# Reordering the first three groups of a gated linear recurrence with an MLP behind it

## The chip, the cores and the metric

The kernel runs on one NeuronCore of a Trainium2 chip. Its time is the device time of one execution in microseconds, as the median of several runs. Five engines work beside each other, each in the order of its own queue: TensorE (PE in the profile, its weight loads PEld), VectorE (DVE), ScalarE (ACT), GpSimd (POOL) and SyncE (SP). SP does no arithmetic here; it issues DMA transfers, one after the other, and a transfer that must wait holds up those behind it.

## The reference

Shapes are fixed: batch 4, 8 heads, 768 steps, head dimension 48. The bridge makes of it 3072 tokens of width 384, and the second block has width 2048.

```python
mag = np.sqrt(a_re * a_re + a_im * a_im)
scale = np.minimum(mag, 0.999) / (mag + 1e-06)
a_re_n, a_im_n = (a_re * scale, a_im * scale)
for t in range(S):
    ar, ai = (a_re_n[:, :, t, :, None], a_im_n[:, :, t, :, None])
    new_re = ar * S_re - ai * S_im
    new_im = ar * S_im + ai * S_re
    kv = np.einsum('bhd,bhe->bhde', k[:, :, t], v[:, :, t])
    S_re, S_im = (new_re + kv, new_im)
    y[:, :, t] = np.einsum('bhd,bhde->bhe', q[:, :, t], S_re)
...
x = np.ascontiguousarray(attn_out.transpose(0, 2, 1, 3)).reshape(B * S, H * D)
h = x @ w_in
g = h * np.cos(h)
return (g @ w_out).astype(np.float32)
```

## The kernel before, in words

The 3072 tokens are cut into 24 chunks of 128 steps, and two chunks make a group: 12 groups, numbered from 0. `PEG` is 2: groups 0 and 1 are handled in one way at two places, the others in another.

For each group the following steps run, in this order of data.

- *Logarithms* (`logs`, `g_log`): ScalarE squares re and im, VectorE adds them into `lg`, then logarithms and exponentials give the log of the gate's size (in `lg`) and the tangent of half its angle (in `tan`). `mag`, `rs` are scratch. `load` fetches re and im of the next group.
- *Products* (`prods`, `g_prod`): a running sum over the 128 steps is a matmul with the constant triangle `sums`; its result is named `lgs`. Two exponentials give P (kept in the tile `lg`) and Q. VectorE forms q times P and k times Q. P's last row is sent to memory (`row`) and read back as a column per head (`end`); SP issues both. `load` fetches k and q of the next group.
- *Angles and phases* (`g_angle`, `g_phase`): an arctangent, then a running sum by matmuls named `phs`, and the whole turns are taken off.
- *Keys* (`keys`, `g_trig`, `g_stack`): sine and cosine, and from them `ks` and `qs`, 96 numbers per head and step.
- *Turning* to kT and qT, which have the 96 numbers on partitions. In groups 0 and 1 TensorE does it (`turned`, `f_turn`, matmuls `tp` against `ident`, copied by ScalarE). In later groups VectorE transposes blocks (`tr`) and DMA does the rest through memory (`moved`, then four transfers kT and one qT).
- *Chunks* (`chunks`): scores `sc` (VectorE masks them into `atm`), the state's update `sp`, and the output of the recurrence. In groups 0 and 1 that is `f_rows` (matmuls `yr`, copied to `rows`) and `f_columns` (three transposes `xp`, copied to xT). In later groups it is `f_out` (matmuls `yp`, two heads side by side, copied to `yT`) and `f_xt`, which turns it by DMA through memory (`x`, then xT).
- *The MLP*: `first` is 48 matmuls `hp` from xT and w_in with a gate each pair on ScalarE and VectorE (`gate`, `junk`); `second(g, i)` is 16 matmuls `op` of chunk i with w_out.

The weights come as 64-bit numbers. `convert` fetches each part by GpSimd's queue and makes 32-bit floats of it: two VectorE steps (L599, L601), one on ScalarE (L603, `low`) and one more on VectorE (L604). There are 12 parts of w_in and 16 of w_out, and they are interleaved with the first groups. In every later group GpSimd and the others check weights for numbers out of range.

The order of work is written down in calls of `weave`. Each takes several lists of steps with two bounds between 0 and 1, spreads each list evenly between its bounds, and runs all steps sorted by place. TensorE's and GpSimd's instructions keep that order, since `chain` makes each follow the last; ScalarE's do for the special functions (`special`), while its other instructions and all of VectorE's and SP's are placed by the scheduler of the language, by readiness. The weaves are: one for group 0's preparation; one with group 0's chunks and its `first`, and group 1's preparation; one with group 0's `second`, group 1's turning, chunks and `first`, and group 2's preparation; and then one for each n from 2, in which group n's chunks, group n-1's `second`, group n+1's preparation and group n's `first` come together.

Of the kernel before, what the change touches and what calls it, by code (L numbers as in the profile page):

```python
# [486 lines left out]
def fast_path(ctx, tc, q, k, v, a_re, a_im, moe_w_in, moe_w_out, out, least, odd, wide):  # L487
# [48 lines left out]
    X = [dict() for _ in range(NG)]  # L536
    Y = [dict() for _ in range(N)]

    PEG = 2

    def load(g, names, i=None):
        for name in names:
# [91 lines left out]
    def matmul(out, **kw):  # L634
        chain(nc.tensor.matmul(out, **kw), "tensor")  # L635

    tables = {AF.Ln: "natural_log_exp_and_others", AF.Exp: "natural_log_exp_and_others",
              AF.Arctan: "trig_and_small", AF.Sin: "trig_and_small"}
    loaded = [None]
# [20 lines left out]
    def g_log(g, i, n):  # L660


        x = X[g]
        re, im = cut(x["re"], i, n), cut(x["im"], i, n)
        if i == 0:
            for name in "lg", "tan", "rs", "mag":
                x[name] = temp(name, 2 if name == "tan" else 1)
        m2, sq, rs, mag = (cut(x[name], i, n) for name in ("lg", "tan", "rs", "mag"))
        nc.scalar.activation(out=m2, in_=re, func=AF.Square)
        nc.scalar.activation(out=sq, in_=im, func=AF.Square)  # L670
        nc.vector.tensor_tensor(out=m2, in0=m2, in1=sq, op=ALU.add)
        special(out=m2, in_=m2, func=AF.Ln, bias=tiny_b)
        special(out=mag, in_=m2, func=AF.Exp, scale=0.5)
        special(out=rs, in_=m2, func=AF.Exp, scale=-0.5)
        nc.vector.scalar_tensor_tensor(out=mag, in0=re, scalar=0.0, in1=mag,
                                       op0=ALU.max, op1=ALU.add)
        nc.vector.tensor_scalar(out=m2, in0=m2, scalar1=0.5, scalar2=math.log(CAP),
                                op0=ALU.mult, op1=ALU.min)
        special(out=rs, in_=rs, func=AF.Ln, scale=EPS, bias=one_b)
        special(out=sq, in_=mag, func=AF.Ln)  # L680
        special(out=sq, in_=sq, func=AF.Exp, scale=-1.0)
        nc.vector.tensor_tensor(out=m2, in0=m2, in1=rs, op=ALU.subtract)  # L682
        nc.vector.tensor_tensor(out=mag, in0=mag, in1=sq, op=ALU.mult)
        nc.vector.scalar_tensor_tensor(out=sq, in0=mag, scalar=2.0, in1=sq,
                                       op0=ALU.subtract, op1=ALU.mult)
        nc.vector.scalar_tensor_tensor(out=sq, in0=sq, scalar=-1.0, in1=im,
                                       op0=ALU.mult, op1=ALU.mult)
        nc.scalar.activation(out=rs, in_=re, func=AF.Relu, scale=-1.0,
                             accum_out=odd[:, ds(next(odds), 1)])

    def g_prod(g, i, n):


        x = X[g]
        if i == 0:
            x["P"], x["Q"] = x["lg"], temp("Q")
            x["row"] = rows_d.tile([G * DM], F32, tag="row", name="row")
            x["end"] = ft.tile([D2, G * H], F32, tag="end", name="end")
        for one in range(i, i + n):
            ps = pa.tile([C, DM], F32, tag="a", name="lgs")  # L700
            matmul(ps, lhsT=sums, rhs=cut(x["lg"], one, 1), start=True, stop=True)
            special(out=cut(x["P"], one, 1), in_=ps, func=AF.Exp)
            special(out=cut(x["Q"], one, 1), in_=ps, func=AF.Exp, scale=-1.0)
        u = cut(x["mag"], i, n)
        P, Q = cut(x["P"], i, n), cut(x["Q"], i, n)
        nc.vector.scalar_tensor_tensor(out=u, in0=Q, scalar=HUGE, in1=P,  # L706
                                       op0=ALU.min, op1=ALU.mult)
# [8 lines left out]
        nc.vector.tensor_scalar(out=end, in0=end, scalar1=-0.5, scalar2=None, op0=ALU.mult)  # L716
# [4 lines left out]
        nc.vector.tensor_tensor(out=P, in0=cut(x["q"], i, n), in1=P, op=ALU.mult)  # L721

    def g_angle(g, i, n):

# [27 lines left out]
    def g_stack(g, i, n):  # L752
        x = X[g]
        if i == 0:
            for name in "ks", "qs":
                x[name] = gt.tile([C, G * H, 2, D], F32, tag=name, name=name)
        for name, product in ("ks", "Q"), ("qs", "P"):
            for a, trig in enumerate(("cos", "sin")):
                nc.vector.tensor_tensor(  # L759
                    out=x[name][:, ds(i * H, n * H), a],  # L760
                    in0=cut(x[product], i, n).rearrange("p (x d) -> p x d", d=D),
                    in1=cut(x[trig], i, n).rearrange("p (x d) -> p x d", d=D), op=ALU.mult)
# [161 lines left out]
    def keys(g):  # L924
# [3 lines left out]
        for i, n in spans(g):  # L928
            yield lambda i=i, n=n: g_trig(g, i, n)
            yield lambda i=i, n=n: g_stack(g, i, n)  # L930
            for name in "kT", "qT":
                if g >= PEG:
                    yield lambda i=i, n=n, name=name: f_transpose(g, i, n, name)
                elif g == 0:
                    yield from turned(g, i, name)

    def turned(g, i, name):
        return [lambda hh=hh: f_turn(g, i, name, hh) for hh in range(2)]
# [14 lines left out]
    def chunks(g):  # L953
        for n in range(g * G, g * G + G):
            for hh in range(2):
                yield lambda n=n, hh=hh: f_scores(n, hh)
            yield lambda n=n: f_state(n)
            yield lambda n=n: f_out(n) if g >= PEG else f_rows(n)
            if g < PEG:
                yield lambda n=n: f_columns(n)  # L960
        if g >= PEG:
            yield lambda: f_xt(g)
        if g + 2 < NG:
            yield lambda: load(g + 2, ("v",))

# [13 lines left out]
    def guarded(g, count):  # L979
# [3 lines left out]
        for _ in range(min(count, len(guards))):  # L983
# [6 lines left out]
    after = stage.tile([1, 1], F32, tag="after", name="after", bufs=1)  # L990
    wait_for(X[0]["im"][0:1, G - 1, 0, 0:1])
    weave((logs(0), 0.0, 0.2), (prods(0), 0.2, 0.4), (each(g_angle, 0), 0.4, 0.5),
          (phases(0), 0.5, 0.6), (keys(0), 0.6, 1.0),
          (convert(into[:6]), 0.2, 1.0))
    weave((chunks(0), 0.0, 0.3), (logs(1), 0.0, 0.1), (convert(into[6:]), 0.0, 0.5),
          (first(0), 0.3, 1.0), (prods(1), 0.55, 0.57), (each(g_angle, 1), 0.58, 0.6),
          (phases(1), 0.75, 0.8), (keys(1), 0.8, 0.9), (convert(back[:8]), 0.5, 1.0))
    weave((convert(back[8:]), 0.0, 0.15), (second(0, 0), 0.0, 0.3),
          ([t for i in range(G) for name in ("kT", "qT") for t in turned(1, i, name)], 0.3, 0.4),
          (logs(2), 0.3, 0.35), (second(0, 1)[:2], 0.4, 0.5), (chunks(1), 0.4, 0.6),  # L1000
          (second(0, 1)[2:], 0.5, 0.6), (prods(2), 0.62, 0.63), (each(g_angle, 2), 0.63, 0.64),
          (first(1), 0.6, 1.0), (phases(2), 0.72, 0.75), (keys(2), 0.76, 0.9))
# [76 lines left out]
```

## Time and profile before

| what | us |
|---|---|
| runs, median (lowest to highest) | 757.03 (755.42 to 759.99) |
| the profiled execution | 759.09 |
| its span, from the first to the last instruction | 757.3 |
| TensorE busy in the span | 698.4 |
| VectorE busy | 397.8 |
| ScalarE busy | 392.3 |

The profiled execution is 2.06 us above the median, and 1.8 us of its time lie outside the span. The mean granted clock of TensorE is 0.972 of full speed. Times in the views are microseconds from the span's start. In the timeline a row has the start, the duration, the engine, the line, the operation, what is written from what, sizes and a count; in brackets stands how long the engine was idle before it, and what ended that. In the chain of work that ended last a row has the start, the duration, and the engine with the tile and line. In the list of waits a row has who waited for whom, the total in us, how often, and the longest. One matmul of 32-bit floats appears in the trace as two instructions, a transpose as one; the listings of the order below count matmuls.

### The profile page before, as it was taken

To read this page: it belongs to the slowest core of one execution; us is meant where nothing else is said; L and a number is where in the kernel's file an instruction comes from. 1 tells how busy PE (TensorE), PEld (TensorE's weight loads), DVE (VectorE), ACT (ScalarE), POOL (GpSimd) and SP (SyncE) were. 2 spreads that over 40 slices of the span, in tenths; PEclk is the share of its full clock that TensorE was granted. 3 is DMA by queue.
4 is the path that set the end of the run, shared out by engine and by line. 5 is a ranking of instruction groups with operands and counts; after the bars stand their busy time and mean duration, and the time that the engine had idled before them with its cause. 6 is when DMAs were issued, how large, how long until landed. Compare 5 with 4: busy or idle time off the path is not lost.

```text
span 757.3 us, 9367 instructions
## 1 busy us (share of the span) xinstructions
PE 698.4 (92%) x3540; PEld 525.3 (69%) x3540; DVE 397.8 (53%) x598; ACT 392.3 (52%) x727; POOL 32.2 (4%) x68
## 2 busy tenths in 40 slices
PE   1489969984999999999999999999999999999996
PEld 0287737773678678678687688687687687687773
DVE  5696972373274464465475366375465556541120
ACT  7485970354337347447557457457456456451230
POOL 2002100000000001001001001001001001000000
PEclk9997998896999999999999999999999999999998
DMA  9855521138244458558566566565574572270100
GB/s 276 200 147 163 150 85 30 35 98 151 73 124 97 115 142 187 122 146 191 121 159 190 120 143 164 116 150 153 116 177 126 126 167 86 62 167 22 43 1 26
DMA packets 231299, 93.96 MB, mean 124 GB/s; under 512 B 208318, under 2 KB 219713, under 8 KB 231244
## 3 DMA queue, kind: packets, MB, share of 16 engines
q1 hardware_dynamic: 224508, 67.76, 41.2%
q0 software_dynamic: 6016, 25.17, 9.6%
q8 instruction: 30, 0.49, 0.3%
q10 hardware_dynamic: 720, 0.33, 0.1%
q14 instruction: 25, 0.20, 0.1%
HBM read 68.82 MB, written 24.42 MB: 123 GB/s over the span
## 4 chain that ended last, share of the span: by engine, by line
PE 81%; DMA 6%; DVE 6%; ACT 3%; SPq 2%; issue 1%; POOL 0%; ACTq 0%; DVEq 0%
PE op L635 32%; PE hp L635 26%; PE sc L635 6%; PE yp L635 5%; PE sp L635 3%; PE phs L635 3%; DMA qT<-moved 3%; PE yr L635 2%; PE lgs L635 2%; SPq L777 1%; PE tp L789 1%; DVE w_out L604 1%; DVE w_out L601 1%; DVE ks L759 1%; DMA moved<-tr 1%
## 5 line engine op out<-in xcount | busy, mean ns | idle before, releaser
L635 PE MATMUL op<-w_out,gate 128*128 128x384 f32 x768 | 269.3, 498 | 3.0 <-DVE w_out L604 3.0
L635 PE MATMUL hp<-xT,w_in 128*128 128x256 f32 x1152 | 254.1, 382 | 0.6 <-ACT xT L850 0.6
L635 PEld LDWEIGHTS hp<-xT,w_in 128*128 128x128 f32 x1152 | 220.7, 192 | 34.6 <-ACT xT L850 1.0
L635 PEld LDWEIGHTS op<-w_out,gate 128*128 128x128 f32 x768 | 144.3, 193 | 101.8 <-DVE w_out L604 8.4
L894 DVE TENSOR_TENSOR gate<-hp,gate 128x512 f32<-128x512 f32 x96 | 65.7, 684 | 119.8 <-ACT gate L645 119.8
L895 ACT ACTIVATE junk<-hp 128x512 bf16<-128x512 f32 x96 | 57.3, 597 | 74.7 <-DVE gate L894 74.5
L645 ACT ACTIVATE gate<-hp,half_pi_b 128x512 f32<-128x512 f32 x96 | 65.6, 684 | 42.6 <-PE hp L635 42.6
L635 PEld LDWEIGHTS sc<-qT,kT 96*128 96x128 f32 x384 | 50.2, 201 | 24.7 <-issue 16.9
L635 PE MATMUL sc<-qT,kT 96*128 96x128 f32 x384 | 52.2, 287 | 15.7 <-DMA qT<-moved 13.9
L706 DVE SCALAR_TENSOR_TENSOR mag<-Q,lg 128x768 f32<-128x768 f32 (+1 forms) x13 | 11.6, 895 | 83.7 <-ACT Q L645 83.7
L808 DVE TENSOR_TENSOR atm<-sc,causal 128x512 f32<-128x512 f32 x48 | 33.0, 688 | 34.1 <-PE sc L635 34.1
L828 ACT COPY yT<-yp 48x512 f32<-48x512 f32 x40 | 23.1, 578 | 51.3 <-PE yp L635 51.0
L738 ACT CAST tan<-phs 128x384 int32<-128x384 f32 x24 | 11.5, 479 | 56.1 <-PE phs L635 56.1
L908 ACT ACTIVATE ot<-op 128x384 f32<-128x384 f32 x24 | 11.6, 483 | 47.1 <-PE op L635 47.1
L644 ACT ACT_TABLE_LOAD x26 | 33.4, 1283 | 3.5 <-issue 3.1
L635 PE MATMUL lgs<-lg,sums 128*128 128x384 f32 x48 | 19.3, 523 | 14.2 <-DVE lg L682 14.2
L635 PE MATMUL yp<-atm,v 128*48 128x128 f32 x320 | 30.4, 277 | 0.0
L635 PEld LDWEIGHTS sp<-v,ks 128*96 128x96 f32 x320 | 29.4, 165 | 0.6 <-issue 0.3
L635 PE MATMUL sp<-v,ks 128*96 128x48 f32 x320 | 29.6, 245 | 0.0
L615 ACT ACTIVATE e<-e,least_e_b 128x384 f32<-128x384 uint32 (+1 forms) x28 | 18.5, 660 | 18.8 <-DVE e L613 18.6
L739 DVE TENSOR_TENSOR tan<-phs,tan 128x384 f32<-128x384 f32 x24 | 13.4, 556 | 27.5 <-ACT tan L738 27.5
L635 PE MATMUL yp<-qT,state 96*48 96x128 f32 x272 | 26.5, 272 | 0.0
(93 smaller groups left out, 710.4 us busy)
## 6 DMA issues: line engine op xcount, KB each, us to landing
moved<-tr SPq DMA_DIRECT2D x20, 768.0 KB
raw<-in_moe_w_in_dram POOLq DMA_DIRECT2D x24, 512.0 KB, 6.1
raw<-in_moe_w_out_dram POOLq DMA_DIRECT2D x32, 384.0 KB, 4.0
kT<-moved SPq DMA_DIRECT2D x40, 192.0 KB
qT<-moved SPq DMA_DIRECT2D x10, 768.0 KB
re<-in_a_re_dram SPq DMA_DIRECT2D x24, 192.0 KB
im<-in_a_im_dram SPq DMA_DIRECT2D x24, 192.0 KB
k<-in_k_dram SPq DMA_DIRECT2D x24, 192.0 KB
```

What stands on the lines that cost most here:

```text
L615: nc.scalar.activation(out=e.bitcast(F32), in_=e, func=AF.Relu, scale=-1.0, bias=least_e_b, accum_out=odd[:, ds(next(odds), 1)])
L635: chain(nc.tensor.matmul(out, **kw), "tensor")
L644: chain(nc.scalar.preload_act_table_set(loaded[0]))
L645: chain(nc.scalar.activation(func=func, **kw))
L706: nc.vector.scalar_tensor_tensor(out=u, in0=Q, scalar=HUGE, in1=P, op0=ALU.min, op1=ALU.mult)
L738: nc.scalar.copy(out=ph.bitcast(I32), in_=ps)
L739: nc.vector.tensor_tensor(out=ph, in0=ps, in1=ph.bitcast(I32), op=ALU.subtract)
L808: nc.vector.tensor_tensor(out=y["atm"][:, ts(hh, HH)], in0=ps, in1=causal.unsqueeze(1).to_broadcast([C, HH, C]), op=ALU.mult)
L828: nc.scalar.copy(out=X[g]["yT"][half, :, i], in_=ps[half])
L894: nc.vector.tensor_tensor(out=gate, in0=ps, in1=gate, op=ALU.mult)
L895: nc.scalar.activation(out=junk, in_=ps, func=AF.Square, scale=1.0 / in_scale, accum_out=wide[:, ds(g * (NJ // 2) + jp, 1)])
L908: nc.scalar.mul(out=ot, in_=ps, mul=1.0 / (in_scale * out_scale))
```

## The change

Five things are changed.

1. `q` times P is written into the tile `mag` and not over P, and `g_stack` reads it there.
2. The two squares of `g_log` are put into ScalarE's chain, so they stay where the weave puts them.
3. `busy(count)` issues matmuls of 128 columns of the constants `ident` and `sums`, whose result nobody reads: six ahead of each of the two `lgs` of group 0, and eight ahead of its turning.
4. Group 1's output goes by `f_out` and `f_xt`, so by DMA; group 0 keeps `f_rows` and `f_columns`. Group 0's steps of turning and of its chunks are written out one by one.
5. The third weave is split in two. In the first half group 1's turning lies between the matmuls of `second(0, 0)`, then come group 1's chunks and in them group 2's products. In the second half `second(0, 1)` and group 2's phases and keys come before `first(1)`.

```diff
+    def busy(count):
+        ps = pa.tile([C, C], F32, tag="a", name="busy")
+        for _ in range(count):
+            matmul(ps, lhsT=ident, rhs=sums, start=True, stop=True)
...
-        nc.scalar.activation(out=m2, in_=re, func=AF.Square)
-        nc.scalar.activation(out=sq, in_=im, func=AF.Square)
+        chain(nc.scalar.activation(out=m2, in_=re, func=AF.Square))
+        chain(nc.scalar.activation(out=sq, in_=im, func=AF.Square))
...
+            if g == 0:
+                busy(6)
             ps = pa.tile([C, DM], F32, tag="a", name="lgs")
...
-        nc.vector.tensor_tensor(out=P, in0=cut(x["q"], i, n), in1=P, op=ALU.mult)
+        nc.vector.tensor_tensor(out=u, in0=cut(x["q"], i, n), in1=P, op=ALU.mult)
...
-        for name, product in ("ks", "Q"), ("qs", "P"):
+        for name, product in ("ks", "Q"), ("qs", "mag"):
...
-            yield lambda n=n: f_out(n) if g >= PEG else f_rows(n)
-            if g < PEG:
-                yield lambda n=n: f_columns(n)
-        if g >= PEG:
-            yield lambda: f_xt(g)
+            yield lambda n=n: f_out(n)
+        yield lambda: f_xt(g)
...
-          (phases(0), 0.5, 0.6), (keys(0), 0.6, 1.0),
-          (convert(into[:6]), 0.2, 1.0))
-    weave((chunks(0), 0.0, 0.3), (logs(1), 0.0, 0.1), (convert(into[6:]), 0.0, 0.5),
-          (first(0), 0.3, 1.0), (prods(1), 0.55, 0.57), (each(g_angle, 1), 0.58, 0.6),
+          (phases(0), 0.5, 0.6), (keys(0), 0.6, 0.9), (convert(into[:6]), 0.2, 1.0))
+    busy(8)
+    for t in (turned(0, 0, "kT") + turned(0, 0, "qT")
+              + [lambda: f_scores(0, 0), lambda: f_scores(0, 1)]
+              + turned(0, 1, "kT") + turned(0, 1, "qT")
+              + [lambda: f_state(0), lambda: f_rows(0), lambda: f_scores(1, 0),
+                 lambda: f_scores(1, 1), lambda: f_columns(0), lambda: f_state(1),
+                 lambda: f_rows(1), lambda: f_columns(1), lambda: load(2, ("v",))]):
+        t()
+    weave((logs(1), 0.0, 0.1), (convert(into[6:]), 0.0, 0.5),
+          (first(0), 0.2, 1.0), (prods(1), 0.55, 0.57), (each(g_angle, 1), 0.58, 0.6),
...
+    over = [t for i in range(G) for name in ("kT", "qT") for t in turned(1, i, name)]
+    weave((convert(back[8:]), 0.0, 0.3), (second(0, 0), 0.0, 0.65), (over, 0.2, 0.6),
+          (logs(2), 0.3, 0.31), (chunks(1), 0.7, 1.0), (prods(2), 0.85, 0.86),
+          (each(g_angle, 2), 0.86, 0.87))
+    weave((second(0, 1), 0.0, 0.35), (phases(2), 0.0, 0.1), (keys(2), 0.1, 0.4),
+          (first(1), 0.4, 1.0))
```

In the changed kernel the lines are some ten further down: L716 becomes L726, L721 becomes L731, L671 becomes L679, L894 becomes L904.

VectorE in group 0, before, from the second half's Q to the first wait for `end`. `mag`, `lg` and Q are the tiles above, and each row of 128x384 is one of the two chunks:

```order
L709 SCALAR_TENSOR_TENSOR Q<-mag,Q 128x384
L604 ISA w_in<-w_in,low 128x1024
L720 TENSOR_TENSOR Q<-k,Q 128x384
L739 TENSOR_TENSOR tan<-phs,tan 128x384
L601 SCALAR_TENSOR_TENSOR w_in<-raw,w_in 128x512
L747 TENSOR_SCALAR cos<-tan 128x384
L721 TENSOR_TENSOR lg<-q,lg 128x384 x2
L604 ISA w_in<-w_in,low 128x1024
L739 TENSOR_TENSOR tan<-phs,tan 128x384
L759 TENSOR_TENSOR ks<-Q,cos 128x8x48
L759 TENSOR_TENSOR ks<-Q,sin 128x8x48
L716 TENSOR_SCALAR end<-end 96x8
```

The same place in the changed kernel:

```order
L749 TENSOR_TENSOR tan<-phs,tan 128x384
L730 TENSOR_TENSOR Q<-k,Q 128x384
L731 TENSOR_TENSOR mag<-q,lg 128x384
L757 TENSOR_SCALAR cos<-tan 128x384
L601 TENSOR_SCALAR w_in<-raw 128x512
L749 TENSOR_TENSOR tan<-phs,tan 128x384
L603 SCALAR_TENSOR_TENSOR w_in<-raw,w_in 128x512
L769 TENSOR_TENSOR ks<-Q,cos 128x8x48
L606 ISA w_in<-w_in,low 128x1024
L769 TENSOR_TENSOR ks<-Q,sin 128x8x48
L769 TENSOR_TENSOR qs<-mag,cos 128x8x48
L726 TENSOR_SCALAR end<-end 96x8
```

The product with q moved up to where it is ready, and one `qs` product now stands ahead of the step on `end`.

TensorE from the `op` matmuls of group 0's first chunk to group 1's scores, before:

```order
L635 MATMUL op<-w_out,gate 128x384 x16
L789 MATMUL tp<-ident,ks 96x128 x8
L789 MATMUL tp<-ident,qs 96x128 x8
L789 MATMUL tp<-ident,ks 96x128 x8
L789 MATMUL tp<-ident,qs 96x128 x8
L635 MATMUL sc<-qT,kT 128x128 x4
```

And in the changed kernel:

```order
L637 MATMUL op<-w_out,gate 128x384 x4
L799 MATMUL tp<-ident,ks 96x128 x4
L637 MATMUL op<-w_out,gate 128x384 x4
L799 MATMUL tp<-ident,ks 96x128 x4
L799 MATMUL tp<-ident,qs 96x128 x8
L637 MATMUL op<-w_out,gate 128x384 x4
L799 MATMUL tp<-ident,ks 96x128 x8
L799 MATMUL tp<-ident,qs 96x128 x4
L637 MATMUL op<-w_out,gate 128x384 x4
L799 MATMUL tp<-ident,qs 96x128 x4
L637 MATMUL sc<-qT,kT 128x128 x8
```

The transposes moved in between the `op` matmuls; four of them are left behind the last.

TensorE around group 1's `hp`, before, from the last transposes of its output to group 2's first scores:

```order
L847 MATMUL xp<-ident,rows 128x128 x3
L635 MATMUL op<-w_out,gate 128x384 x4
L635 MATMUL lgs<-lg,sums 128x384 x2
L635 MATMUL hp<-xT,w_in 128x256 x18
L635 MATMUL phs<-tan,turns 128x384
L635 MATMUL phs<-tan,last 128x384
L635 MATMUL phs<-tan,turns 128x384
L635 MATMUL phs<-tan,last 128x384
L635 MATMUL hp<-xT,w_in 128x256 x30
L635 MATMUL sc<-qT,kT 128x128 x4
```

And in the changed kernel, from the last `yp` of group 1 (its `lgs` stand between the two halves of the scores before):

```order
L637 MATMUL yp<-qT,state 48x128 x2
L637 MATMUL phs<-tan,turns 128x384
L637 MATMUL phs<-tan,last 128x384
L637 MATMUL op<-w_out,gate 128x384 x4
L637 MATMUL phs<-tan,turns 128x384
L637 MATMUL phs<-tan,last 128x384
L637 MATMUL op<-w_out,gate 128x384 x12
L637 MATMUL hp<-xT,w_in 128x256 x48
L637 MATMUL sc<-qT,kT 128x128 x4
```

Group 2's `phs`, and all of the `op` of group 0's second chunk, now stand ahead of the whole of `hp`.

SP's queue at the same place, before, from group 2's `row` on:

```order
L712 DMA row<-lg 1x768
L715 DMA end<-row 48x16x1 x2
L549 DMA k<-in_k_dram 128x8x48 x2
L549 DMA q<-in_q_dram 128x8x48 x2
L774 DMA moved<-tr 128x1536 x2
L777 DMA kT<-moved 96x16x32 x4
L779 DMA qT<-moved 96x4x512
```

And in the changed kernel:

```order
L722 DMA row<-lg 1x768
L885 DMA x<-yT 48x4x256
L551 DMA k<-in_k_dram 128x8x48
L725 DMA end<-row 48x16x1 x2
L551 DMA k<-in_k_dram 128x8x48
L551 DMA q<-in_q_dram 128x8x48 x2
L885 DMA x<-yT 48x4x256
L551 DMA v<-in_v_dram 128x8x48
L889 DMA xT<-x 128x3x256
L784 DMA moved<-tr 128x1536
```

The two halves of group 1's output, `x`, came in around the loads of k and q, and xT after them.

More of the change, by code (lines that the diff above doesn't have):

```diff
@@ L537, in fast_path @@
     Y = [dict() for _ in range(N)]
-    PEG = 2
+    PEG, PER = 2, 1
     def load(g, names, i=None):
@@ L933, in keys @@
                     yield lambda i=i, n=n, name=name: f_transpose(g, i, n, name)
-                elif g == 0:
-                    yield from turned(g, i, name)
     def turned(g, i, name):
@@ L992, in fast_path @@
     weave((logs(0), 0.0, 0.2), (prods(0), 0.2, 0.4), (each(g_angle, 0), 0.4, 0.5),
-          (phases(0), 0.5, 0.6), (keys(0), 0.6, 1.0),
-          (convert(into[:6]), 0.2, 1.0))
-    weave((chunks(0), 0.0, 0.3), (logs(1), 0.0, 0.1), (convert(into[6:]), 0.0, 0.5),
-          (first(0), 0.3, 1.0), (prods(1), 0.55, 0.57), (each(g_angle, 1), 0.58, 0.6),
-          (phases(1), 0.75, 0.8), (keys(1), 0.8, 0.9), (convert(back[:8]), 0.5, 1.0))
[L998 to L1002, printed above, removed]
+          (phases(0), 0.5, 0.6), (keys(0), 0.6, 0.9), (convert(into[:6]), 0.2, 1.0))
[9 more added lines that the diff above has]
+          (first(0), 0.2, 1.0), (prods(1), 0.55, 0.57), (each(g_angle, 1), 0.58, 0.6),
+          (phases(1), 0.75, 0.8), (keys(1), 0.8, 0.9), (convert(back[:8]), 0.5, 1.0))
+    over = [t for i in range(G) for name in ("kT", "qT") for t in turned(1, i, name)]
[4 more added lines that the diff above has]
+          (first(1), 0.4, 1.0))
     for n in range(2, NG):
```

## The prediction

> **What bounds the kernel now.** I read the busy time by stretches first (columns: stretch in us, its length, busy us and instructions of TensorE, its weight loads, VectorE, ScalarE, GpSimd, then granted clock, DMA share, GB/s), with the stretches cut where TensorE's order changes kind.
>
> ```profile
> 24.20:30.09 5.89, 0.88 (x2) 0.00 (x0) 0.05 (x1) 0.00 (x0) 0.53 (x1) 1.00 1.11 246
> 30.09:61.30 31.21, 22.55 (x150) 21.15 (x150) 28.11 (x54) 22.14 (x36) 3.85 (x7) 0.92 0.52 130
> 61.30:89.40 28.10, 27.76 (x108) 22.25 (x109) 21.98 (x44) 22.12 (x42) 5.54 (x9) 0.90 0.66 179
> 89.40:104.30 14.90, 12.02 (x32) 5.00 (x30) 14.90 (x32) 9.44 (x16) 1.61 (x3) 1.00 0.31 98
> 104.30:111.90 7.60, 4.73 (x35) 3.74 (x35) 3.79 (x6) 7.57 (x14) 0.00 (x0) 0.96 0.07 26
> 111.90:144.40 32.50, 31.93 (x170) 25.17 (x171) 6.57 (x10) 4.69 (x11) 0.00 (x0) 0.80 0.19 38
> 144.40:168.70 24.30, 23.77 (x105) 19.49 (x103) 18.00 (x22) 15.68 (x31) 0.00 (x0) 1.00 0.29 71
> 168.70:181.70 13.00, 0.00 (x0) 0.01 (x1) 7.58 (x10) 8.97 (x14) 0.00 (x0) 0.65 1.13 210
> 181.70:757.30 575.60, 567.77 (x2934) 425.81 (x2934) 281.39 (x385) 284.70 (x536) 16.04 (x35) 0.99 0.50 120
> ```
>
> From 181.70 on TensorE is busy 567.8 of 575.6 us, and what it lacks lies after its last matmul. So TensorE bounds that part, and the change leaves its order there as it was. All that can move is when group 2's first `sc` starts, 181.73 now. Before it stand a front in which VectorE and ScalarE stop (24.20 to 30.09), a stretch in which VectorE has no free time (89.40 to 104.30, the conversions of w_out), and 13 us without a matmul. The waits of TensorE, then the front in order of time, then VectorE's waits between 34 and 104.3 and the last conversion say what ends each:
>
> ```profile
> PE lgs L635 <- DVE lg L682: 14.2, 2, 10.3
> PE sc L635 <- DMA qT<-moved: 13.9, 3, 13.0
> PE tp L789 <- DVE ks L759: 12.0, 2, 8.9
> ```
>
> ```profile
> 30.09 1.03 DVE L721 TENSOR_TENSOR lg<-q,lg 128x384 f32<-128x384 f32 x2 [5.84 <-DMA row<-lg]
> 30.73 0.84 ACT L670 ACTIVATE tan<-im 128x768 f32<-128x768 f32 x1 [7.49 <-DMA im<-in_a_im_dram]
> 33.84 0.16 DVE L716 TENSOR_SCALAR end<-end 96x8 f32<-96x8 f32 x1
> 33.98 1.94 PE L789 MATMUL tp<-ident,ks 128*96 128x128 f32 x8 [8.90 <-DVE ks L759]
> 34.46 0.55 DVE L759 TENSOR_TENSOR qs<-lg,sin 128x384 f32<-128x384 f32 x1
> 44.16 3.01 PE L635 MATMUL sc<-qT,kT 96*128 96x128 f32 x16
> 61.32 9.03 PE L635 MATMUL hp<-xT,w_in 128*128 128x256 f32 x28 [0.57 <-ACT xT L850]
> ```
>
> ```profile
> DVE gate L894 <- ACT gate L645: 4.9, 1, 4.9
> ```
>
> ```profile
> 104.37 0.91 PE L635 MATMUL op<-w_out,gate 128*128 128x384 f32 x2 [0.89 <-DVE w_out L604]
> 106.00 1.04 PE L789 MATMUL tp<-ident,qs 128*96 128x128 f32 x8
> ```
>
> **Front.** L721 wrote q times P over P, so it waited for the transfer that still read P. L670, the square of the next group's im, stood on ScalarE ahead of group 0's phase work and waited 7.49 us for its load. With a tile of its own and the squares chained behind, both stops go. What is late next is L726, which waits for the small transfer `end`. Its `row` is issued behind loads on SP that the change does not touch, so I leave it at 33.84. In the new order the last product `qs` stands right behind it: 33.84+0.16+0.55 is 34.6. Eight transposes at 1.04 to 1.94 us and a copy give `sc` at about 36 to 37, where before it came at 44.16, since it now goes ahead of the second chunk's transposes. From `sc` to the first `hp` took 17.2 us (44.16 to 61.32). The second chunk's 16 transposes now lie inside (2 to 4 us), but the same instructions at full clock save about as much. First `hp`: 53, against 61.32. The conversions that VectorE now does before the second half's logarithms push that half back some 4 us, under the wait for `end`.
>
> The constants are 20 matmuls of 128 columns, 40 instructions. At 3.01/16 = 0.19 us that is 7.5 us, in waits of 14.2 and 12.0 us, and no input waits for them. They cost nothing and may raise the clock.
>
> **To the last conversion.** VectorE's work is the same, and it ends the conversions at 104.3. From 30.09 to there it is free for 3.1+6.1+0 us. With some 2 us of work done earlier, the end could come at 94; with nothing regained, at 104.3. I take 102, near the upper row: the 4.9 us of the wait for the first gate shrink, but the new order still has gates, `end` and a whole group's logarithms ahead of the w_out conversions, each waiting on other engines. So of 8 us gained at the front, 6 are lost here.
>
> **Transposes of group 1.** All 32 now stand between the `op` matmuls that wait for conversions, so behind the last `op` (0.65) only four transposes (0.45) remain. `sc` of group 1 starts at 103.1, against 111.9. Their ScalarE copies now interleave with the conversions' ScalarE step, which leaves 14.90-9.44 = 5.5 us free there; in the next stretch before, the copies and a group's logarithms together took 7.57.
>
> **Group 1 and its output.** The rates come from the chain that ended last, in group 2 and later:
>
> ```profile
> 194.57 1.79 PE sc L635 x16
> 242.70 1.32 PE sp L635 x16
> 198.94 1.90 PE yp L635 x32
> 203.61 1.29 PE lgs L635 x4
> 213.28 1.29 PE phs L635 x4
> 204.90 5.16 PE op L635 x16
> 217.16 20.72 PE hp L635 x96
> ```
>
> From `sc` to the first `hp` of group 1 now stand, on TensorE, 32 `sc` (3.58), 32 `sp` (2.64), 64 `yp` (3.80), 4 `lgs` (1.29), 8 `phs` (2.58) and 32 `op` (10.32): 24.2 us, against 32.5. The 64 `yr` and 6 `xp` are gone, and with them a stretch whose granted clock is 0.80. So `hp` could start at 127.3, if xT is there. It now comes by DMA:
>
> ```profile
> 209.69 0.95 DVE L721 TENSOR_TENSOR lg<-q,lg 128x768 f32<-128x768 f32 x1
> 212.04 1.39 SPq L549 DMA_DIRECT2D q<-in_q_dram  x2
> 697.00 1.86 SPq L875 DMA_DIRECT2D x<-yT  x2
> 701.16 0.38 SPq L879 DMA_DIRECT2D xT<-x  x1
> ```
>
> ```profile
> 154.83 0.91 PE phs L635 x2
> 166.18 3.25 DMA moved<-tr
> 174.41 7.23 DMA qT<-moved
> 181.73 2.04 PE sc L635 x8
> 183.77 3.91 PE op L635 x8
> ```
>
> On SP the second half of x is now queued behind `k`, `end`, `k` and two `q` loads, and `q` waits for L731. `lgs` would end at 103.1+1.79+1.32+1.90+0.89+1.29 = 110.3. In group 3 the product of L721 ends at 210.64, 5.7 us after `lgs` (204.90); here the two `state` steps and an `atm` come between, so some 7.5: 117.8. Two q issues (1.39) put x at 119.2. No row gives the landing of x or xT; the nearest are `moved`, 3.25 us, and qT, 7.23 us, both through the same memory and larger or as large. The last group's two steps, 697.00 and 701.16, show the first within 4.2 us with its issues, near the lower one. So xT lands between 125.7 and 133.7. With 3.25 for x and 5, midway, for the strided xT it is 127.5, and a v load stands between them on SP. I take a wait of 1.3 us: `hp` at 128.6, ends 0 and 6.4. Behind xT on SP stand `moved`, kT and qT of group 2, whose `tr` is not ready before; it holds nothing up.
>
> **The 13 us.** Phases, keys and transposes of group 2 now come ahead of `hp` of group 1, which stays 20.72 us long without the `phs` inside. From the end of the last `phs` (155.74) to the landing of qT (181.64) took 25.9 us with gates between. Now the last `phs` ends at 110.3+0.89+1.32+1.90+2.58+2.58 = 119.6, so qT lands by 145.5, while TensorE reaches `sc` at 128.6+20.7 = 149.3. The stall is gone, with 3.8 us to spare; the cover is `hp` plus three quarters of an `op`.
>
> **Sum.** `sc` of group 2 at 149.3 instead of 181.73. The first instructions after the stall also ran slow: 2.04 us for 8 `sc` (0.90 at the rate above) and 3.91 for 8 `op` (2.58), 2.5 us that go too. 757.3-32.4-2.5 = 722.4 span. The profiled execution took 1.8 us more than its span and lies 2.1 us above the median of 757.03: predicted median 722.
>
> Steady groups: the squares, add and `mag` product change places but not number; L731's output no longer holds `lg`. I cost this at nothing: a group's `lgs` starts 13 us after its input L682 is done:
>
> ```profile
> 244.28 0.95 DVE L682 TENSOR_TENSOR lg<-lg,rs 128x768 f32<-128x768 f32 x1
> 258.27 1.29 PE lgs L635 x4
> ```
>
> **Rivals.** (a) *TensorE stays at half clock in the front.* Speaking for it: 1.94 us for 8 transposes at 33.98 against 1.04 at 106.00, and the clock falls to 0.92 and 0.90 around group 0's `yr`. Then the first `hp` comes at 58 to 60, the conversions end at 104 to 108, and the median is 724 to 728. The Trainium skill ("TensorE: Matmul & The Clock Gate", Part 1: The HAM clock gate) says that the array starts at half clock and is released only by some 3.4 us of sustained activity. By that rule 6 constants, 12 x 0.19 = 2.3 us, and 8, 3.0 us, are each too short to do it alone, and (a) would hold, 727; the trace agrees so far that 3.85 us of transposes at 33.98 did not release it. (b) *xT is late.* With 7.23 us for both steps `hp` waits 6.4 us: 727. Against it: the same two steps never stopped TensorE in ten later groups, though behind 40 `op` and 4 `lgs` where here 32 `op` stand. (c) *VectorE regains its free time*: conversions end at 96, 716. (d) *The stall moves and stays*: if the way from `phs` to qT takes over 29.7 us, each us more is lost; back in full it gives 735. Against it: for group 3 the way fits between the last `phs` (214.57) and the end of `hp` (237.88), 23.3 us, and the waits for qT other than the 13.0 add up to 0.9.
>
> (e) *Slower than before*: the squares now behind the last gate lengthen every group's logarithms by 2 x 0.84 + 0.95 = 2.6 us, and VectorE's add stands between the two `atm` products, so that `yp` could wait in each of 10 groups. The way to `lgs` decides only from 13 us more; to undo 35 us the add must cost `yp` 3.5 us a group, more than the 2.6 us that it is late.
>
> **Chances.** The forecast 0.55 (its own range 718 to 726), (a) 0.18, (b) 0.1, (c) 0.1, (d) 0.04, (e) 0.03. Range 713 to 731: it takes in (a), (b) and (c). A difference under 0.5%, 3.8 us, cannot be told here from no change; faster 0.96, same 0.01, slower 0.03.
>
> **What would show it.** VectorE has no wait for `row` and its wait for `end` ends near 33.8; first `hp` near 53; the last `op` of group 0 that waits for w_out near 102; no `yr` after 60; `hp` of group 1 at 127 to 130, with a wait named xT or none; no wait on `qT` at group 2's first `sc`, near 149; 573 us from there to the end. The forecast is wrong if `sc` of group 2 is not between 141 and 158, or if waits appear on TensorE after it.

## Result: 727.1 us against 756.2, and the profile after

The changed kernel takes 727.06 us (median; 725.74 to 727.43), the kernel before beside it 756.22 (755.41 to 759.99). The ratio is 0.960, interval 0.957 to 0.964: faster by 29 us. The forecast was 722, range 713 to 731. The profiled execution took 726.93 us, 725.1 of them in the span.

The stretches again, with the columns of the first table of the prediction, cut where TensorE's order changes kind:

```profile
24.20:31.00 6.80, 5.23 (x23) 3.14 (x23) 6.41 (x15) 4.30 (x8) 0.53 (x1) 0.82 0.98 208
31.00:37.30 6.30, 2.74 (x17) 2.19 (x17) 2.75 (x10) 2.49 (x5) 0.00 (x0) 0.70 0.88 179
37.30:56.65 19.35, 18.21 (x136) 17.51 (x135) 12.74 (x23) 12.92 (x20) 1.60 (x3) 0.76 0.31 89
56.65:82.40 25.75, 21.34 (x82) 16.84 (x82) 23.12 (x41) 21.13 (x39) 4.31 (x8) 0.90 0.64 166
82.40:91.00 8.60, 8.57 (x26) 6.74 (x27) 7.73 (x17) 4.74 (x8) 1.61 (x3) 0.67 0.83 206
91.00:104.98 13.98, 13.09 (x60) 8.43 (x59) 13.93 (x32) 12.93 (x24) 2.15 (x4) 1.00 0.34 114
104.98:106.17 1.19, 1.19 (x7) 0.86 (x8) 0.00 (x0) 1.16 (x2) 0.00 (x0) 1.00 0.00 0
106.17:130.76 24.59, 24.59 (x175) 18.28 (x174) 21.03 (x29) 13.55 (x23) 0.00 (x0) 1.00 0.58 122
130.76:151.48 20.72, 20.72 (x98) 18.24 (x97) 7.12 (x9) 10.12 (x22) 0.00 (x0) 1.00 0.68 162
151.48:725.10 573.62, 564.71 (x2935) 424.43 (x2933) 287.62 (x393) 292.35 (x550) 16.04 (x35) 1.00 0.50 121
```

The stretch without a matmul is gone: from 106.17 to 151.48 TensorE has no idle time. Group 2's first `sc` comes at 151.48, against 181.73, so 30.25 us of the 32.2 that the span lost are gained ahead of it; the rest lies in the slow start behind the old stall. But the last `op` that waits for w_out stands at 104.98, where it stood at 104.37 before. Up to there the change gained nothing, although the first `hp` comes 4.7 us earlier. The waits and the timeline rows that belong to it:

```profile
PE phs L637 <- DVE tan L749: 3.9, 1, 3.9
PE tp L799 <- DVE qs L769: 3.6, 1, 3.6
PE sc L637 <- DMA qT<-moved: 0.9, 2, 0.7
PE op L637 <- DVE w_out L606: 0.9, 1, 0.9
```

```profile
34.85 0.17 DVE L726 TENSOR_SCALAR end<-end 96x8 f32<-96x8 f32 x1 [3.55 <-DMA end<-row]
35.53 1.94 PE L799 MATMUL tp<-ident,qs 128*96 128x128 f32 x8 [3.56 <-DVE qs L769]
37.30 3.78 PE L637 MATMUL sc<-qT,kT 96*128 96x128 f32 x16
56.65 5.55 PE L637 MATMUL hp<-xT,w_in 128*128 128x256 f32 x15 [0.57 <-ACT xT L860]
82.42 1.65 PE L637 MATMUL phs<-tan,last 128*128 128x384 f32 x2 [3.92 <-DVE tan L749]
104.98 0.91 PE L637 MATMUL op<-w_out,gate 128*128 128x384 f32 x2 [0.89 <-DVE w_out L606]
106.17 1.95 PE L637 MATMUL sc<-qT,kT 96*128 96x128 f32 x16
```

VectorE waits for `end`, TensorE waits for the product that stands behind it there (35.53) and runs at half clock (16 `sc` in 3.78 us, where 1.95 is the time at 106.17). At 82.42 it waits 3.9 us for a small VectorE step.

### The profile page after: what moved, and what is told of

It reads as the page before. It is cut to its first block, busy times and chain, and to the rows that moved or that the text cites. A ratio compares the mean times of both kernels' runs of the same rounds, so it can differ in the third digit from the quotient of the medians.

```text
span 725.1 us, 9428 instructions
## 1 busy us (share of the span) xinstructions
PE 689.0 (95%) x3574; PEld 523.1 (72%) x3574; DVE 396.3 (55%) x598; ACT 393.3 (54%) x728; POOL 31.4 (4%) x68
## 4 chain that ended last, share of the span: by engine, by line
PE 85%; DMA 6%; DVE 5%; ACT 1%; issue 1%; SPq 1%; POOL 0%; DVEq 0%
PE op L637 33%; PE hp L637 29%; PE sc L637 6%; PE yp L637 5%; PE sp L637 4%; PE phs L637 4%; DMA qT<-moved 2%; PE lgs L637 2%; DMA end<-row 1%; DVE w_out L606 1%; DVE w_out L603 1%; PE yr L637 1%; PE tp L799 1%; DMA raw<-in_moe_w_in_dram 1%; DMA im<-in_a_im_dram 1%
## 5 line engine op out<-in xcount | busy, mean ns | idle before, releaser
L637 PE MATMUL op<-w_out,gate 128*128 128x384 f32 x768 | 262.6, 489 | 0.9 <-DVE w_out L606 0.9
L637 PEld LDWEIGHTS op<-w_out,gate 128*128 128x128 f32 x768 | 142.3, 190 | 95.0 <-issue 3.7
L904 DVE TENSOR_TENSOR gate<-hp,gate 128x512 f32<-128x512 f32 x96 | 65.6, 684 | 135.3 <-ACT gate L653 135.3
L716 DVE SCALAR_TENSOR_TENSOR mag<-Q,lg 128x768 f32<-128x768 f32 (+1 forms) x13 | 11.6, 895 | 63.5 <-ACT Q L653 63.5
L838 ACT COPY yT<-yp 48x512 f32<-48x512 f32 x44 | 25.4, 578 | 38.6 <-PE yp L637 37.9
L637 PE MATMUL yp<-atm,v 128*48 128x128 f32 x352 | 33.5, 277 | 0.0
L637 PE MATMUL yp<-qT,state 96*48 96x128 f32 x304 | 29.6, 272 | 0.0
```

Of the source, the lines that this page charges most:

```text
L838: nc.scalar.copy(out=X[g]["yT"][half, :, i], in_=ps[half])
L904: nc.vector.tensor_tensor(out=gate, in0=ps, in1=gate, op=ALU.mult)
```

## Experiments

Two theories stood against each other at first. *A*: the order of VectorE's work sets the last `op` at 105, whatever the front does, and all of the gain comes from the later half of the change. *B*: TensorE's half clock in the front costs the 5 us that the forecast lacks. All kernels are compared with runs of the kernel before on the same chip.

**The constants alone.** The changed kernel without them:

```diff
-            if g == 0:
-                busy(6)
...
-    busy(8)
```

> The changed kernel without the 20 matmuls on constants. Theory A: what sets the end of group 0's output matmuls (last `op` that waits for w_out at 105.0) is VectorE, whose order of work holds the conversions; the constants change TensorE's clock only where it waits anyhow. Then the first `hp` stays within 1 us of 56.7, the last `op` within 1 us of 105.0, and the median is 726 to 729. Theory B: TensorE's clock in the front is what the end lacks; then the transposes of ks (1.08 us for 8 now) take 1.9, the whole front runs at half clock, `hp` starts 2 to 3 us later and so does all behind it: 729 to 732.

Measured: 725.87 us (724.10 to 728.20), not told apart from 727.06. The first `hp` came at 53.46, 3.2 us earlier and not later, and the last wait for w_out ended at 101.52, 3.5 us earlier. So the constants bring nothing. A has the median nearly right and both places wrong; B is wrong in the median and in `hp`. Of the 3.5 us, 1.8 were lost again later: from group 2's first `sc` (148.01) to the end it took 575.4 us, where the changed kernel takes 573.6, with waits for qT of 2.6 us in all where that has 0.9. Why is open.

**The two halves of the change.** First the kernel before with parts 4 and 5 for group 1 alone (its output by DMA, the third weave of the changed kernel), then the changed kernel with just these undone:

```diff
 # the later half alone, on the kernel before
-            yield lambda n=n: f_out(n) if g >= PEG else f_rows(n)
-            if g < PEG:
+            yield lambda n=n: f_out(n) if g >= 1 else f_rows(n)
+            if g < 1:
                 yield lambda n=n: f_columns(n)
...
+    over = [t for i in range(G) for name in ("kT", "qT") for t in turned(1, i, name)]
...
```

> The kernel before, with the later half of the change alone: group 1's output by DMA, group 1's 32 transposes between the last `op` of group 0, group 2's phases and keys ahead of group 1's `hp`. The front is as before (first `hp` near 61.3, where the whole change has 56.7). Theory A, VectorE's conversions end near 104.4 whatever the front does: group 1's `sc` at 105.6, group 2's 45.3 us later at 150.9, median 725 to 727, so the front's half of the change is worth nothing. Theory B, the front's 4.7 us reach the end: last `op` near 109, median 730 to 732.

> The changed kernel with the later half undone: group 1's output through rows and transposes again and the order of the third stretch as before; the front is the changed one. Theory A: first `hp` at 56.7 but the last `op` near 105, group 1's `sc` at 112 to 113, the 13 us without a matmul back: median 755 to 758, no gain against before. Theory B: the front's 4.7 us reach the end: 750 to 753.

The later half alone takes 726.19 us (725.97 to 729.10; ratio to before 0.960, interval 0.957 to 0.963), as much as the whole change. The front's half alone takes 757.79 (ratio 1.000, 0.996 to 1.003): nothing. In the first, `hp` starts at 59.24 and the last wait for w_out ends at 102.69; in the second `hp` starts at 53.82 and that wait ends at 103.17. The first two rows are of the later half alone, the other two of the front's half:

```profile
59.24 10.69 PE L635 MATMUL hp<-xT,w_in 128*128 128x256 f32 x36 [0.57 <-ACT xT L850]
102.69 0.91 PE L635 MATMUL op<-w_out,gate 128*128 128x384 f32 x2 [0.90 <-DVE w_out L604]
53.82 13.31 PE L637 MATMUL hp<-xT,w_in 128*128 128x256 f32 x48 [0.57 <-ACT xT L860]
103.17 0.91 PE L637 MATMUL op<-w_out,gate 128*128 128x384 f32 x2 [0.89 <-DVE w_out L606]
```

An `hp` 5.4 us earlier thus left the last `op` where it was. The medians are those of A, and B's, 730 to 732 and 750 to 753, are out. A's places were off by 2 to 3 us: it had the last `op` near 104.4 and 105, and `hp` at 56.7 in the second kernel.

**Less work for VectorE.** From the changed kernel, the VectorE instruction that puts the sign in is left out of the conversions of w_out; its output is then another one.

```diff
-        nc.vector.scalar_tensor_tensor(out=bits, in0=hi, scalar=0xC0000000, in1=bits,
-                                       op0=ALU.bitwise_and, op1=ALU.bitwise_or)
+        if n == W:
+            nc.vector.scalar_tensor_tensor(out=bits, in0=hi, scalar=0xC0000000, in1=bits,
+                                           op0=ALU.bitwise_and, op1=ALU.bitwise_or)
```

> The changed kernel, with one of the three VectorE instructions of each w_out conversion left out (the one that puts the sign in, 16 times 0.47 us from start to start, 7.5 us; so the output is another one). Theory A: VectorE's load before 105 falls by 7.5 us, its product `tan` that TensorE's `phs` waits 3.9 us for comes 1 to 2 us earlier, the last `op` ends its wait at 98 to 101: median 720 to 723. Theory B, TensorE at half clock bounds: the wait of 0.9 us for w_out goes and nothing else, 725.5 to 727.

Measured: 729.39 us (727.46 to 731.69), no faster than the changed kernel (ratio to before 0.964, 0.961 to 0.967, where that has 0.960 and, repeated, 0.962), though A's step came true: the last `op` ended at 101.14 and not 105.89. The gain was given back right behind it. From `sc` to the first `hp` of group 1 it took

```profile
101.41:131.25 29.84, 28.23 (x174) 21.32 (x173) 20.09 (x27) 13.82 (x24) 0.00 (x0) 0.89 0.48 101
105.20:112.02 6.82, 6.78 (x50) 6.30 (x51) 3.85 (x6) 1.68 (x4) 0.00 (x0) 0.50 0.66 144
```

where the changed kernel has 24.59 at a clock of 1.00. The second row is the part of it at half clock. TensorE now waits 0.73 and 0.88 us for ScalarE's copies of the transposes, 1.6 us, and then runs 6.8 us at half clock, some 3.4 us lost; together nearly the 5.2.

**Constants against that.** The last kernel, with matmuls on constants at the two waits:

```diff
                 yield lambda n=n, hh=hh: f_scores(n, hh)
+                if n == G:
+                    yield lambda: busy(4)
```

> The kernel with the lighter VectorE again (the sign instruction of 16 w_out conversions left out), with four matmuls on constants behind each half of group 1's first `sc`. Without them that kernel brought the last `op` 3 to 5 us forward and lost it between `sc` and the first `hp` of group 1, 29.8 us against 24.6, with a granted clock of a half from 105.2 to 112.0. Theory C, the clock took it: the constants fill the waits of 0.7 and 0.9 us ahead of that stretch, the clock stays full, `sc` to `hp` takes 25 to 26.5, median 724.5 to 727. Rival, ScalarE's late copies of the transposes took it: 28.5 or more and 728.5 to 731.

Measured: 727.14 us (726.76 to 730.54), and 30.1 us from `sc` to `hp`. The constants stood behind the same copy, since their tile comes from the same buffers:

```profile
102.90 1.16 PE L638 MATMUL busy<-sums,ident 128*128 128x128 f32 x8 [0.74 <-ACT kT L802]
104.94 2.07 PE L638 MATMUL sc<-qT,kT 96*128 96x128 f32 x8 [0.88 <-ACT kT L802]
```

They filled neither wait. The half-clock stretch became 3.4 us instead of 6.8, and the constants took what that gave. The stretch is as the rival had it (28.5 or more), the median lies just above that of C. This tells nothing on whether a full clock alone would have kept the gain.

**The later half in its three parts**, each undone by itself in the changed kernel: group 1's output through `yr` and `xp` again; group 2's phases and keys among group 1's `hp` again; group 1's transposes behind the `op` again.

```diff
 # output through rows
-            yield lambda n=n: f_out(n)
+            yield lambda n=n: f_out(n) if g >= PEG else f_rows(n)
...
 # phases late
-    weave((second(0, 1), 0.0, 0.35), (phases(2), 0.0, 0.1), (keys(2), 0.1, 0.4),
-          (first(1), 0.4, 1.0))
+    weave((second(0, 1), 0.0, 0.35), (first(1), 0.4, 1.0),
+          (phases(2), 0.58, 0.625), (keys(2), 0.64, 0.85))
 # transposes late
-    weave((convert(back[8:]), 0.0, 0.3), (second(0, 0), 0.0, 0.65), (over, 0.2, 0.6),
+    weave((convert(back[8:]), 0.0, 0.15), (second(0, 0), 0.0, 0.3), (over, 0.3, 0.6),
```

> The changed kernel with one part undone: group 1's output goes through `yr` and `xp` on TensorE again, as before, in place of `yp` and the two DMA steps. Theory L (the gain is the sum of three parts of the later half, each worth what its stretch of the trace before shows): from `sc` to the first `hp` of group 1 it takes 32.5 us again in place of 24.6, with a granted clock near 0.8, so 8 us more: median 733 to 736. Rival: only the instructions count, 64 `yr` and 6 `xp` at full clock against 64 `yp`, 3 to 4 us: 730 to 731.5.

> The changed kernel with one part undone: group 2's phases and keys stand among group 1's `hp` again, not ahead of them. Theory L: the way from the last `phs` to the landing of qT, 25.9 us before, is covered by only 30 `hp`, 13 us, so TensorE stands still for some 13 us again and starts slowly behind it (2.5 us): median 741 to 745. Rival: the shorter queue on SP and the cleared VectorE shorten that way below 20 us, and the wait is under 7 us: 731 to 736.

> The changed kernel with one part undone: group 1's 32 transposes stand behind the last `op` of group 0's first chunk again, not between the `op` that wait for the conversions. Theory L: those `op` wait for w_out again (about 4 us in all) and the transposes with their copies come behind the last of them, so group 1's `sc` comes 5 to 7 us later: median 732 to 735. Rival: since in the changed kernel the last `op` waits only 0.9 us for w_out, TensorE has no time to spare there and the order costs nothing but the copies' latency, 1 to 2 us: 727 to 729.

| undone | median (range), us | over the repeated changed kernel (727.13) |
|---|---|---|
| output through rows | 734.34 (733.73 to 736.76) | 7.2 |
| phases late | 749.26 (748.79 to 751.70) | 22.1 |
| transposes late | 738.38 (737.22 to 739.72) | 11.3 |

The stretch from `sc` to `hp` of group 1 with the rows back, what opens ahead of `hp` and of group 2's `sc` with the phases late, and the stretches ahead of `sc` and to `hp` with the transposes late:

```profile
104.89:139.33 34.44, 33.30 (x180) 25.55 (x179) 21.14 (x29) 13.27 (x23) 0.00 (x0) 0.85 0.34 64
```

```profile
PE sc L637 <- DMA qT<-moved: 12.8, 1, 12.8
PE hp L637 <- DMA xT<-x: 4.1, 1, 4.1
```

```profile
107.01:113.62 6.61, 3.81 (x33) 3.10 (x30) 4.24 (x5) 6.61 (x13) 0.00 (x0) 1.00 0.08 30
113.62:143.11 29.49, 29.49 (x174) 22.82 (x173) 17.64 (x25) 10.60 (x18) 0.00 (x0) 0.83 0.47 95
```

The first gave the time expected: 9.9 us more at a clock of 0.85, less 1.3 from an earlier `sc`. The second was too small in theory L by 4 us: the 13 us came back, but `xT` now also stops TensorE, since the `phs` no longer stand ahead of `hp`. That is rival (b) of the prediction, which the phases had been covering. The third too: 6.6 us of transposes and copies ahead of `sc`, and 4.9 more behind it at a clock of 0.83. The three sum to 40.6 us and not to 29. They are not independent: each one undone opens waits and half-clock stretches that were closed with all three in place.

**The changed kernel again.**

> The changed kernel, nothing altered, for a second profile. Theory C: the first `hp` at 56.65 was a matter of where the clock's steps fell in that execution, since three relatives had it at 53.3 to 53.8; here it is again near 53.5, and the last `op` that waits for w_out near 102. Rival: 56.7 and 105 again, and the relatives owe their 3 us to their edits. The median is 725 to 728 either way.

Measured: 727.13 us (726.39 to 728.42); `hp` at 56.07, the last `op` ended at 105.63. So the forecast of C, an `hp` near 53.5 again, did not come true. But C is not out. Six profiles run TensorE in the same order up to 90 us, and VectorE and ScalarE too: two of the changed kernel, that of the front's half, and three with one part undone. In three of these `hp` came at 56.65, 56.07 and 56.78, in the others at 53.82, 54.27 and 54.09, so executions of one order do differ by 2 to 3 us there. Four of the six keep the order up to the last `op`: with `hp` at 56.65 and 56.07 it came at 104.98 and 104.72, with `hp` at 54.27 and 54.09 at 103.71 and 103.87, so about half of such a difference reaches it. What the profiles share is when `end` lands: among the eight profiles with the changed front up to here, VectorE's wait for it ended at 34.85, 34.28 and 35.03 in the three with `hp` at 56.1 to 56.8, and at 32.8 to 34.0 in the five with `hp` at 53.3 to 54.3. In the three the granted clock was a half from 33.5, 33.1 and 35.4 us on, for 6.8 to 10.2 us; in the five it was full from 36.3 us at the latest to 49.8. Why the landing differs is open.

**Another order.** Three edits together: the two small VectorE steps on `end` are emitted behind the first scores, three conversions of w_in are brought into the first chunk's work, and an `hp` stands between group 1's two phase steps.

```diff
+        if g > 0:
+            g_end(g, i, n)      # the scaling of `end` and the step on `least`, in a function
...
+              + [lambda: f_scores(0, 0), lambda: f_scores(0, 1)] + each(g_end, 0)
...
+    weave((middle, 0.0, 1.0), (convert(into[6:9]), 0, 1))
+    weave((logs(1), 0.0, 0.1), (convert(into[9:]), 0.0, 0.5),
...
-          (phases(1), 0.75, 0.8), (keys(1), 0.8, 0.9), (convert(back[:8]), 0.5, 1.0))
+          (phases(1), 0.75, 0.95), (keys(1), 0.9, 1.0), (convert(back[:8]), 0.5, 1.0))
```

> The changed kernel in another order: the two small VectorE steps on `end` stand behind the first scores, three conversions of w_in move from behind the first chunk's work into it, and an `hp` stands between group 1's two phase steps. Theory A, the order of VectorE's work is what holds the last `op` at 105 (VectorE stands still for some 13 us between 31 and 105, and TensorE for 3.9 in front of `phs`): the wait of 3.5 us for `end` and that of 3.9 go, the last `op` comes at 99 to 102: median 722 to 725. Rival, whatever comes early there is given back between `sc` and `hp` of group 1, as with the lighter VectorE: 726 to 730.

> The same order without the 20 matmuls on constants. If they do nothing for the end, as their removal alone showed (725.9 against 727.1, within the scatter), this is within 1.5 us of the run with them: 722 to 726 by theory A. If they pay once `end` no longer stops TensorE right behind them, this is 2 to 3 us slower than with them.

> The changed kernel with one of the three edits of the better order: an `hp` stands between group 1's two phase steps, and its keys come behind. Theory A in its strict form, VectorE's order alone holds the last `op` at 105: TensorE no longer waits 3.9 us in front of `phs` and no longer falls to half clock behind it, but then waits longer for w_out; the last `op` stays at 104 to 106, median 725.5 to 728. Rival, that wait and the half clock behind it (some 3.9 + 3.0 us) are themselves what held it: the last `op` at 99 to 101, median 720 to 723. In between, both count.

The three edits: 719.05 us (four runs at 718.29 to 719.51, two at 724.73 and 725.34), ratio to before 0.951 (0.947 to 0.954), better than the changed kernel's 0.960 and, repeated, 0.962 (0.960 to 0.963), and better than the 722 to 725 of A. Without the constants 721.43 (720.80 to 723.72), ratio 0.952 (0.949 to 0.954), not told apart; group 2's first `sc` comes at 143.55 without them and 143.71 with them. The phases apart alone 725.84 (723.54 to 726.97). Its wait did not go but stands 1 us later, so this run does not decide between A and its rival; in the timeline of that kernel, and the same step in the kernel with all three:

```profile
83.45 1.65 PE L637 MATMUL phs<-tan,last 128*128 128x384 f32 x2 [4.28 <-DVE tan L749]
```

```profile
78.79 0.81 PE L637 MATMUL phs<-tan,turns 128*128 128x384 f32 x2
79.43 0.81 PE L637 MATMUL phs<-tan,last 128*128 128x384 f32 x2
```

Where TensorE stands in the order did not matter, since VectorE came to `tan` late. The stretch from 31 to 100 us shows what changed: before, changed, phases apart, all three edits (the third number pair is VectorE):

```profile
31.00:100.00 69.00, 59.59 (x282) 47.52 (x282) 59.78 (x119) 51.71 (x89) 11.01 (x19) 0.93 0.56 152
```

```profile
31.00:100.00 69.00, 59.86 (x296) 49.20 (x297) 55.34 (x110) 50.24 (x87) 9.68 (x18) 0.83 0.58 152
```

```profile
31.00:100.00 69.00, 58.71 (x298) 47.69 (x299) 56.05 (x111) 50.88 (x88) 10.09 (x18) 0.88 0.59 152
```

```profile
31.00:100.00 69.00, 60.94 (x337) 49.22 (x338) 62.94 (x125) 56.67 (x98) 10.96 (x19) 0.95 0.57 152
```

VectorE stands still for 9.2, 13.7, 12.9 and 6.1 us there. Of the changed kernel's 13.7 us, 4.4 are waits for `end`, and 3.1 the wait for `sp`, which TensorE computed late, at half clock. In the front's half, the same order there with the clock full from 28.6 to 52.5 us, that wait is 0.3 us. The row of the changed kernel, then that of the front's half:

```profile
DVE state L877 <- PE sp L637: 3.1, 1, 3.1
DVE state L877 <- PE sp L637: 0.3, 1, 0.3
```

So the half clock of B is one source of VectorE's idle time, and the two theories do not exclude each other. With the three edits the last `op` of group 0 ends at 98.12 with no wait for w_out, and what follows keeps its length:

```profile
98.39:122.98 24.59, 24.59 (x174) 18.31 (x173) 20.97 (x29) 13.24 (x22) 0.00 (x0) 1.00 0.58 121
122.98:143.71 20.73, 20.73 (x98) 18.30 (x97) 7.14 (x9) 10.11 (x22) 0.00 (x0) 1.00 0.67 162
```

Nothing of the 7.8 us at `sc` is given back. That is as A has it: less idle time of VectorE, an earlier last `op`. But the first `hp` came at 51.28 here, 5.4 us earlier, at a clock of 0.95 over the stretch instead of 0.83, so these runs do not part VectorE's order from TensorE's earlier start. How much each of the other two edits gave was not tried.

## Why the prediction held, point by point

The time lies in the range, but above the forecast's own 718 to 726. Of the 5.1 us over 722, 2.7 are in the span: 3.1 at group 1's `sc` and 0.5 behind group 2's, less 0.9 between. Another 2.2 are the last term of the sum: the profiled execution before lay 2.1 us above its median, and the new one lies 0.1 below. That 2.1 us was taken over as if it belonged to the kernel. What is left is rounding.

- **The stall of 13 us and the slow start behind it** (right). `sc` of group 2 was put 46.2 us behind that of group 1 (103.1 to 149.3); it took 45.3. From there to the end 573.1 was forecast, 573.6 measured. The steady groups cost nothing more, so rival (e) is out, and undoing the phases alone brought the stall back at 12.8 us.
- **Group 1's output** (right in sum). 24.2 us from `sc` to `hp` was forecast, 24.59 measured, and 34.4 with `yr` and `xp` back. Its wait of 1.3 us for xT did not come; with 0.4 us more in the stretch that is the 0.9 us less. SP reached the second half of x later than forecast, 123.58 and not 119.2, behind the same loads, but from there `xT` was issued 3.5 us later, and it landed in about 3 us and not 5, by the experiment in which TensorE waited for it (issued at 128.25, `hp` at 131.32). It was just in time: `hp` starts 3.7 us after the issue in the changed kernel.

```profile
123.58 0.84 SPq L885 DMA_DIRECT2D x<-yT  x1
127.05 0.37 SPq L889 DMA_DIRECT2D xT<-x  x1
130.76 20.88 PE L637 MATMUL hp<-xT,w_in 128*128 128x256 f32 x96
```

- **Transposes of group 1** (right). 1.1 us from the last wait for w_out to `sc` was forecast, 1.2 measured.
- **Front** (too optimistic by 3.7 us). The two stops named went, and the next one was the one named, `end` (34.85 against 33.84). The step that failed is "the same instructions at full clock save about as much": the granted clock fell to a half at 33.5, while TensorE waited for `end`, and again at 54.0 in the small `yr` matmuls. `sc` came at 37.30, where 53 less 17.2 is 35.8, and from there to `hp` it took 19.35 us and not 17.2, so `hp` came at 56.65.
- **To the last conversion** (too optimistic by 3.0 us, the largest part of the miss). The term "I take 102" was the mis-sized one: 104.98, the upper bound named, 104.3, and 0.7 more. The front half alone (757.8) shows that its worth was zero, not 2 us. I had counted VectorE's free time of before as time to be had; the changed order has more of it from 31 to 100 us, 13.7 us against 9.2.
- **The constants**, costed at nothing: no cost and no gain that these runs can tell.
- **Rival (a)** gave 724 to 728, and the time lies there, and so do the conversions (104 to 108), but `hp` does not (58 to 60). Half the mechanism is there: the clock did fall ahead of `sc`. But its sum, late `hp` makes late conversions, holds for about half of the delay within one order, and not from one order to another: the later half alone has `hp` at 59.24 and the same time.

The rule that was drawn from the Trainium skill for that rival ("TensorE: Matmul & The Clock Gate", Part 1) made the constants too short to release the clock alone. Here the granted clock by stretch, where the third column from the end counts:

```profile
13.03:16.44 3.41, 0.70 (x6) 0.51 (x5) 3.32 (x8) 2.35 (x4) 0.53 (x1) 1.00 1.04 389
16.44:26.68 10.24, 4.54 (x7) 1.75 (x7) 9.90 (x22) 9.04 (x19) 1.06 (x2) 0.50 1.09 334
26.68:33.51 6.83, 3.72 (x27) 3.01 (x26) 4.57 (x10) 3.78 (x7) 0.53 (x1) 1.00 0.92 192
33.51:43.75 10.24, 8.22 (x38) 7.78 (x39) 7.37 (x18) 5.78 (x9) 1.06 (x2) 0.50 0.58 135
43.75:53.99 10.24, 10.24 (x102) 10.24 (x100) 6.81 (x12) 6.58 (x10) 0.54 (x1) 1.00 0.19 67
53.99:60.82 6.83, 5.69 (x17) 4.29 (x17) 4.46 (x7) 5.22 (x8) 0.54 (x1) 0.50 0.55 109
```

The clock was released at 13.0, behind `lgs` and constants without a pause, and lost again in the wait that followed. The release at 26.7 was not theirs: it came behind `phs`, and the eight constants start at 27.37. In the second profile of this kernel the first record of a full clock stands at 26.3 us, though the constants are the same. The window of some 3.4 us that the same part of the Trainium skill gives agrees with the lengths here, 3.41, 6.83 and 10.24 us, which are one, two and three of it. So a released clock followed on the constants in one of two profiles, at a place where no long matmuls came next.

## What to carry to other kernels

Before counting a gain at the front of a pipelined start, find the engine whose queue carries the work that the next stage waits for last, and ask whether the earlier start lessens that engine's idle time. Here that grew from 9.2 to 13.7 us, and an `hp` 4.7 us earlier came to nothing. A half of a change that is run by itself tells more than the whole: the two halves showed that all of it came from the later part. And prices of parts undone one by one need not add up, since each part may be the cover of another.

## What the runs showed of the hardware

- The granted clock falls without a long wait: at 54.0 us in the changed kernel TensorE had been busy for all of the 10.24 us before (the row from 43.75), at its end with 48-column `yr` matmuls, and the next 15 `hp` instructions took 5.55 us.
- In the kernel with the lighter VectorE two waits of under 0.9 us were followed by 6.8 us at half clock. Its `sc` came 4.8 us earlier than in the changed kernel (101.41 against 106.17), its `hp` 0.5 us later (131.25 against 130.76).
- Issued from 29.9 to 31.2 us, the small transfer of `end` ended VectorE's wait anywhere from 32.8 to 35.0 us in eight profiles: issued from 30.03 on it ended at 34.85 in one, issued from 30.09 on at 32.82 in another.
